# Summing two of three exponential words in GpSimd's accumulating transfers, and a plan without its table

## The chip, the cores and the metric

The kernel runs on one core of a Trainium2 chip. The metric is the device time of one execution in microseconds. Before the change it is 1371.47 us, the median of two runs (1370.7 and 1372.23).

## The reference

Two layers, each of attention and a ReLU feed-forward block, with the same weights in both layers. The sequence has 2048 rows of 512 columns, and there are 32 heads of 16 columns. The feed-forward width is 1792.

```
qkv = (x @ wqkv).reshape(B, S, 3, H, Dh).transpose(2, 0, 3, 1, 4)
q, k, v = qkv[0], qkv[1], qkv[2]
scores = jnp.einsum("bhqd,bhkd->bhqk", q, k) * (Dh ** -0.5)
p = _softmax(scores, axis=-1)
o = jnp.einsum("bhqk,bhkd->bhqd", p, v)
A = o.transpose(0, 2, 1, 3).reshape(B, S, D) @ wo
B = maximum(x @ w1, 0) @ w2

x = x + A(layernorm(x)); x = x + B(layernorm(x))
x = x + A(layernorm(x)); x = x + B(layernorm(x))
```

## The kernel before

**Blocks and slots.** The work of attention is cut into blocks: one head, 128 keys, 512 queries. There are 2 x 4 x 32 x 16 = 4096 of them (chunks of the last layer are narrower, and two or four narrow ones make one block). A slot takes three blocks (W = 3): TensorE writes their scores side by side into one of two PSUM tiles `ps_s` (L1946), and ScalarE takes the exponential of what is in the tile and writes it to a buffer `e` in SBUF (L1959). With 4096 blocks there are 1366 slots.

**Two ways to an exponential.** In a slot, the third block can be left to VectorE. Then ScalarE's exp is 1024 columns wide instead of 1536. VectorE's way uses that the bits of a bf16 number, read as an integer, are nearly its logarithm. One instruction (`first_step`, L1478) adds a bias to the scores and writes them as 16-bit integers into a buffer `lin`. Two such blocks make a pair (GROUP = 2) of 1024 columns in one `lin` buffer. GpSimd then makes two shifted copies with 64-bit integer adds (`shifted`, L1533): `up`, a constant added to each word, and `down`, the constant subtracted. Read as bf16, the sum `lin + up + WEIGHT * down` is close to a multiple of the exponential. The sum is never written: TensorE multiplies each of the three with the values, and adds in PSUM. The weight of `down` lies in scaled copies of the values (`vscaled`, for six of the sixteen key blocks), or is multiplied in by VectorE (`weigh`, L1537).

**Value products.** A product (`pv`, L1299) has 32 output rows, so that four heads' products run side by side, and sums go to one of two PSUM tiles `ps_f` and `ps_o`. A block of ScalarE's takes one product, a block of VectorE's three (PARTS = lin, up, down). When a head group's sums are complete (`finish_segment`), VectorE copies them out; the reciprocal of the softmax's denominator is spread over the rows by transfers of SP and, where there is time, of GpSimd (`widen`, L1253: 64 rows read from four).

**Fillers and repeats.** Projections, transposes and the feed-forward block are cut into small pieces that TensorE does between scores and value products (L429 and others). Where TensorE would stand idle, the scores of a slot are issued more than once (`times`).

**What sets the order.** All instructions are written out in one order by a planner in the kernel's Python. It keeps a clock for each engine (`now_pe`, `now_dve`, `now_pool`, `exp_end`) with assumed costs, and for each slot decides whether VectorE takes a block (only if a `lin` buffer is free, `lin_free`, and GpSimd's queue allows it), which products and fillers TensorE does before the next scores, and when each task of VectorE and GpSimd is issued. A dictionary `rule` holds thresholds of these decisions. A table corrects it: `STARTS` (whether a slot begins a pair), `MORE` and `SLIP` (more fillers, or a shifted limit, in a slot) and `RULES` (new thresholds from a slot on). On the chip each engine follows its own queue in this order and waits for semaphores.

**Buffers.** There are NP = 6 `lin` buffers, NC = 3 of `up` and ND = 4 of `down`. In the old kernel a `lin` buffer is free when both shifts have read it and the value products of `lin` are done; `up` and `down` when their products are done.

Of the kernel before, what the change touches and what calls it, by code (L numbers as in the profile page):

```python
# [12 lines left out]
BF16 = mybir.dt.bfloat16  # L13
# [5 lines left out]
ALU = mybir.AluOpType  # L19
# [7 lines left out]
def kernel(  # L27
# [10 lines left out]
    nc = tc.nc  # L38
# [11 lines left out]
    NKB = S // P  # L50
# [3 lines left out]
    TPC = QS // P  # L54
# [16 lines left out]
    GROUP = 2  # L71
    CHAIN = 1500.0
    NP = 6
    NC = 3
# [15 lines left out]
    CROWDED, POOL_ISSUE, BEHIND = 4500.0, 700.0, 3500.0  # L90
    LOADED, FIRST_LOAD, LATER_LOAD, KEPT_Q = 18000.0, 30, 180, 8
    BOTH = 4
    WHOLE = 4
    STARTS, MORE, SLIP = {27: 0, 33: 0, 22: 0, 38: 1, 52: 0, 57: 0, 61: 0, 79: 0, 98: 0, 100: 1, 103: 1, 107: 1, 128: 1, 136: 0, 158: 1, 193: 0, 220: 1, 239: 0, 221: 0, 260: 1, 242: 1, 251: 0, 249: 0, 305: 1, 301: 1, 325: 1, 323: 1, 351: 0, 368: 1, 366: 0, 392: 1, 401: 1, 402: 0, 418: 0, 405: 1, 438: 1, 456: 0, 477: 1, 516: 0, 505: 1, 533: 1, 526: 0, 595: 1, 659: 0, 642: 0, 681: 0, 693: 0, 710: 0, 708: 0, 740: 1, 753: 0, 755: 1, 746: 0, 749: 0, 769: 0, 765: 1, 799: 1, 806: 0, 815: 1, 830: 1, 838: 0, 829: 0, 869: 1, 866: 0, 873: 1, 880: 0, 883: 0, 881: 1, 907: 1, 902: 0, 953: 0, 960: 0, 985: 0, 991: 0, 1026: 0, 1046: 0, 1068: 0, 1079: 0, 1067: 1, 1076: 1, 1096: 0, 1128: 0, 1125: 0, 1126: 0, 1156: 0, 1158: 0, 1178: 1, 1164: 0, 1189: 0, 1254: 1, 1280: 0, 1370: 0}, {8: 1.0, 2: -1.0, 15: -1.0, 28: 2.0, 42: -1.0, 80: 2.0, 72: -1.0, 95: 1.0, 92: 1.0, 87: -1.0, 156: 1.0, 166: -1.0, 207: 2.0, 223: 2.0, 234: -1.0, 287: 2.0, 318: -1.0, 407: 1.0, 437: 2.0, 495: -1.0, 486: 2.0, 520: 2.0, 533: 1.0, 564: 1.0, 572: 2.0, 577: 1.0, 594: -1.0, 589: 2.0, 599: -1.0, 620: 2.0, 624: 2.0, 649: -1.0, 660: 2.0, 643: 2.0, 669: -1.0, 683: -1.0, 712: 2.0, 736: 2.0, 735: 2.0, 738: 1.0, 741: 2.0, 758: 2.0, 757: 1.0, 786: 2.0, 784: 1.0, 814: 2.0, 819: 1.0, 839: 1.0, 861: 1.0, 874: 1.0, 865: -1.0, 886: 1.0, 897: 1.0, 892: 2.0, 953: 2.0, 955: 1.0, 941: 1.0, 1000: -1.0, 1022: 2.0, 1028: 2.0, 1033: 1.0, 1061: 1.0, 1119: -1.0, 1117: -1.0, 1112: 1.0, 1181: 1.0, 1205: -1.0, 1220: 1.0, 1221: -1.0, 1241: -1.0, 1255: -1.0, 1250: -1.0, 1276: 2.0, 1281: -1.0, 1326: 1.0, 1335: 2.0, 1357: 2.0, 1341: 2.0, 1347: 2.0}, {54: 216.0, 82: -200.0, 141: 216.0, 168: -200.0, 176: 120.0, 180: -200.0, 194: 120.0, 221: 120.0, 249: 120.0, 241: 216.0, 247: 60.0, 279: 120.0, 278: -200.0, 277: 216.0, 282: 216.0, 309: 120.0, 329: 120.0, 355: 216.0, 377: 120.0, 409: 120.0, 432: 120.0, 524: -200.0, 547: 216.0, 552: 216.0, 544: 120.0, 580: 216.0, 616: 60.0, 612: -200.0, 603: -200.0, 644: 60.0, 722: 120.0, 723: -200.0, 730: 60.0, 777: 120.0, 766: 60.0, 763: 60.0, 784: 216.0, 785: -200.0, 792: 216.0, 803: 60.0, 815: 60.0, 819: -200.0, 835: -200.0, 825: 216.0, 830: -200.0, 887: -200.0, 918: -200.0, 909: 216.0, 903: 216.0, 946: 216.0, 951: 120.0, 958: -200.0, 991: 60.0, 1044: 216.0, 1042: -200.0, 1057: 120.0, 1069: 120.0, 1071: 216.0, 1073: 60.0, 1111: 60.0, 1159: 60.0, 1200: 120.0, 1187: 60.0, 1196: 216.0, 1216: 120.0, 1238: 60.0, 1298: 120.0, 1313: 60.0, 1315: -200.0, 1304: -200.0, 1344: 120.0, 1362: -200.0, 1373: 120.0, 1365: 120.0}
# [8 lines left out]
    RULES = {1: {'pressed': 5, 'young': 6}, 21: {'backlog': 4000.0}, 41: {'unit': 360.0, 'pressed': 3, 'hold': 4, 'over': 0.0, 'calm': 1.5, 'cap': 10.0, 'fill': 2000.0, 'rounds': 4}, 61: {'full': 3}, 81: {'unit': 280.0, 'cap': 6.0, 'late': 99.0, 'spare': 10}, 101: {'slack': 300.0, 'fill': 2000.0}, 121: {'margin': 160.0, 'most': 2.0}, 141: {'eager': 0, 'hold': 4, 'late': 3.0, 'rounds': 3, 'pressed': 5, 'margin': 130.0, 'over': 0.0, 'partial': 3}, 161: {'full': 2}, 181: {'full': 2, 'ahead': 3.0, 'calm': 2.0, 'pace': 1.5, 'unit': 320.0, 'partial': 3, 'least': 0.5, 'most': 2.0}, 201: {'far': 2, 'pressed': 3, 'most': 2.0, 'least': 0.5, 'easy': 1.2, 'calm': 3.0, 'near': 8, 'rounds': 4}, 221: {'spare': 20, 'ahead': 3.0, 'calm': 1.2, 'haste': 2.0, 'hold': 4, 'pace': 1.3, 'cap': 3.0, 'young': 4}, 241: {'hold': 4, 'most': 50.0, 'ahead': 5.0, 'haste': 3.0}, 261: {'pressed': 5}, 281: {'cap': 3.0, 'least': 1.0, 'margin': 100.0, 'full': 2}, 301: {'far': 3, 'late': 99.0, 'pressed': 4, 'cap': 3.0, 'backlog': 2200.0, 'calm': 9.0, 'eager': 1, 'unit': 360.0}, 321: {'backlog': 2200.0, 'far': 3, 'eager': 0, 'cap': 6.0, 'unit': 320.0, 'over': 60.0, 'calm': 2.0, 'spare': 14}, 361: {'easy': 1.0, 'late': 2.0}, 381: {'cap': 3.0, 'slack': 300.0}, 401: {'eager': 0, 'pace': 0.7}, 421: {'calm': 9.0, 'old': 4}, 441: {'partial': 2, 'cap': 6.0, 'calm': 1.0, 'fill': 3000.0}, 461: {'pressed': 5}, 481: {'easy': 2.0, 'rounds': 3, 'cap': 10.0, 'pace': 1.0}, 501: {'haste': 1.6, 'ahead': 1.0, 'slack': 300.0, 'least': 1.0}, 521: {'margin': 100.0, 'unit': 360.0}, 541: {'cap': 3.0}, 561: {'closing': 3, 'full': 4}, 581: {'young': 6}, 621: {'partial': 2, 'late': 4.0}, 641: {'ahead': 3.0, 'calm': 1.0}, 661: {'far': 4, 'backlog': 3000.0}, 681: {'calm': 1.2, 'soon': 2000.0, 'unit': 360.0, 'hold': 2, 'far': 2, 'easy': 1.2, 'eager': 1, 'full': 3}, 701: {'young': 4, 'hold': 4}, 721: {'least': 1.0, 'pace': 0.7, 'backlog': 4000.0, 'fill': 3000.0}, 761: {'hold': 2, 'full': 3, 'closing': 6, 'haste': 2.0}, 821: {'over': 120.0, 'partial': 4}, 861: {'pace': 1.5, 'rounds': 3}, 881: {'spare': 6, 'far': 4}, 901: {'backlog': 3000.0}, 941: {'young': 3, 'pace': 1.0, 'far': 4, 'backlog': 3000.0, 'slack': 800.0, 'late': 99.0, 'partial': 2, 'pressed': 5}, 981: {'far': 4, 'slack': 800.0}, 1021: {'ahead': 8.0, 'pace': 0.7, 'rounds': 4, 'near': 6, 'far': 2, 'late': 2.0, 'backlog': 1500.0, 'full': 2}, 1041: {'margin': 60.0, 'young': 4}, 1061: {'margin': 100.0}, 1101: {'old': 4}, 1121: {'rounds': 4}, 1161: {'late': 99.0}, 1201: {'unit': 360.0, 'most': 50.0, 'calm': 1.5, 'over': 200.0, 'full': 4, 'least': 0.5, 'closing': 0, 'cap': 10.0}, 1221: {'margin': 160.0}, 1241: {'calm': 9.0, 'unit': 320.0}, 1261: {'hold': 4}, 1281: {'over': 120.0, 'backlog': 2200.0, 'least': 1.0, 'late': 99.0}, 1301: {'pace': 1.0, 'least': 0.5}, 1321: {'pressed': 4, 'slack': 1300.0}, 1341: {'calm': 1.2, 'unit': 320.0, 'far': 2, 'fill': 2000.0}, 1361: {'slack': 1300.0}}  # L103
# [1015 lines left out]
    for l in range(2):  # L1119


        if l == 0:
            steps = [(0, range(4), 0, TPC), (0, range(4), TPC, 2 * TPC), (0, range(4), 2 * TPC, NKB)]
            steps += [(j, range(4), 0, NKB) for j in range(1, NQS)]
        else:
            steps = [(0, range(4), 0, NKB - TPC), (1, range(NEXT), 0, NKB - TPC)]
            steps += [(0, range(4), NKB - TPC, NKB), (1, range(NEXT, 4), 0, NKB)]
            steps += [(1, range(NEXT), NKB - TPC, NKB)]
            steps += [(j, range(4), 0, NKB) for j in range(2, LAST + 1)]
        for j, Ts, a, b in steps:  # L1130
            for T in Ts:
                sums = acc[8 * j :] if l else acc0
                add_run(l, j, T, range(a, b), load=a and sums, store=b < NKB and sums)
# [246 lines left out]
    def v_round(found, t):  # L1380
# [19 lines left out]
        for p in list(pairs):  # L1400
# [5 lines left out]
            for half in range(GROUP):  # L1406
                line = ("line", p["n"], half)
                if ("read",) + line not in made and not any(x[4] == line for x in p["mms"]):
                    mark(("read",) + line, "pe")
# [57 lines left out]
    PARTS = ("lin", "up", "down")  # L1467
# [5 lines left out]
    def dve_block(half, taken, src, ex, recent):  # L1473
# [27 lines left out]
        for sg, kb, g in taken:  # L1501
# [9 lines left out]
            for part, buf, key, of in (  # L1511
                ("lin", lin[which], line_key, None),
                ("up", up[p["n"] % NC], p["key"] + ("up",), None),
# [7 lines left out]
    def chain(p):  # L1521
# [19 lines left out]
        for of, out, by, war in (  # L1541
# [7 lines left out]
            maker[key + of]["chain"] = p  # L1549
        if not p["scaled"]:  # L1550
            task(quick, weigh, [key + ("down",)], [key + first])
            maker[key + ("down",)]["chain"] = p
# [11 lines left out]
    idle_matmuls(16)  # L1564
# [630 lines left out]
```

## Time and profile before

| what | value |
|---|---|
| profiled execution, its own time | 1371.6 us |
| its span | 1369.8 us |
| TensorE busy | 1333.9 us (97%) |
| ScalarE busy | 1344.5 us (98%) |
| VectorE busy | 1145.0 us (84%) |
| GpSimd busy | 765.7 us (56%) |
| granted TensorE clock | 1.0 |

The span runs from the first to the last instruction of the execution that the profiler recorded. Busy times are unions over the span; issuing a transfer counts as busy on GpSimd, where the profile gives it a length. Four products that run side by side count as one stretch. TensorE's busy time includes the repeated scores. In the rows of groups, a mean length of an exp is longer than the time from one exp to the next, because the end of one overlaps the start of the next.

### The profile page before, as it was taken

What the parts mean: (1) busy time and instruction counts of PE and PEld (TensorE: products, weight loads), DVE (VectorE), ACT (ScalarE), POOL (GpSimd) and SP (SyncE); (2) the same over time, 40 slices, a digit from 0 to 9 for tenths busy, and PEclk for the clock granted to TensorE, in tenths of its full rate; (3) what the DMA queues carried; (4) which work ended last, traced back from release to release, by engine and by line L of the source; (5) the groups of instructions that cost most, each with busy time, mean ns of one, the idle gap of its engine ahead of it and who ended that gap; (6) DMA issues with size and microseconds to landing.
All of it is one profiled execution on the core that took longest, in us unless ns stands there. A gap on an engine that the chain in (4) does not pass through costs nothing. (4 is left out here: it accounts for less than half of the span.)

```text
span 1369.8 us, 48788 instructions
## 1 busy us (share of the span) xinstructions
PE 1333.9 (97%) x20647; PEld 470.5 (34%) x20647; DVE 1145.0 (84%) x1994; ACT 1344.5 (98%) x1437; POOL 765.7 (56%) x1296
## 2 busy tenths in 40 slices
PE   8999999999999999999999999999999999999998
PEld 3222222222222222222222222222234444545665
DVE  7898998869998889986898877998988886887774
ACT  8999999999999999999999999999999999999995
POOL 3456666546566655664566544565545555565441
PEclk9999999999999999999999999999999999999999
DMA  6200012101022100210111100002112211214120
GB/s 148 70 2 14 21 43 45 47 16 33 11 49 48 23 21 6 56 42 18 25 21 32 33 5 6 11 15 52 41 35 51 50 28 38 65 30 96 35 58 19
DMA packets 151579, 50.03 MB, mean 37 GB/s; under 512 B 136608, under 2 KB 148576, under 8 KB 151360
## 3 DMA queue, kind: packets, MB, share of 16 engines
q1 hardware_dynamic: 144832, 41.31, 13.4%
q0 software_dynamic: 5568, 5.15, 2.0%
q8 instruction: 161, 2.64, 0.8%
q10 hardware_dynamic: 960, 0.46, 0.1%
q14 instruction: 58, 0.48, 0.1%
HBM read 24.38 MB, written 2.10 MB: 19 GB/s over the span
## 5 line engine op out<-in xcount | busy, mean ns | idle before, releaser
L1959 ACT ACTIVATE e<-ps_s 128x1024 bf16<-128x1024 f32 (+1 forms) x1366 | 1330.2, 1172 | 6.9 <-PE ps_s L1946 5.1
L1478 DVE TENSOR_SCALAR lin<-ps_s 128x512 int16<-128x512 f32 x1200 | 802.4, 684 | 154.8 <-PE ps_s L1946 116.5
L1533 POOL INT64_ADD up<-lin x600 | 367.6, 617 | 425.6 <-DVE lin L1478 220.7
L1946 PE MATMUL ps_s<-q,ktp 32*128 32x512 bf16 (+2 forms) x5460 | 523.3, 321 | 12.5 <-ACT e L1959 7.6
L1533 POOL INT64_ADD down<-lin x600 | 368.1, 617 | 130.8 <-DVE lin L1478 46.8
L1946 PEld LDWEIGHTS <-ktp 32*128 32x128 bf16 x5728 | 166.5, 91 | 509.4 <-issue 501.1
L1299 PEld LDWEIGHTS <-vaug 128*32 128x32 bf16 x7338 | 178.6, 95 | 196.0 <-issue 167.1
L1299 PE MATMUL ps_o<-e,vaug 128*32 128x512 bf16 (+2 forms) x2094 | 201.3, 321 | 2.6 <-DVE ht L1163 0.8
L1299 PE MATMUL ps_f<-e,vaug 128*32 128x512 bf16 (+2 forms) x1922 | 198.3, 330 | 1.4 <-DVE q L914 0.8
L1299 PE MATMUL ps_f<-lin,vaug 128*32 128x512 bf16 (+2 forms) x766 | 113.8, 332 | 0.1
L1299 PE MATMUL ps_f<-down,vscaled 128*32 128x512 bf16 (+2 forms) x728 | 113.5, 329 | 0.0
L1299 PE MATMUL ps_f<-up,vaug 128*32 128x512 bf16 (+2 forms) x766 | 113.1, 332 | 0.0
L1299 PE MATMUL ps_o<-up,vaug 128*32 128x512 bf16 (+2 forms) x850 | 110.2, 322 | 0.0
L1299 PE MATMUL ps_o<-lin,vaug 128*32 128x512 bf16 (+2 forms) x850 | 105.6, 322 | 0.5 <-DVE ht L1161 0.3
L1299 PE MATMUL ps_o<-down,vscaled 128*32 128x512 bf16 (+2 forms) x798 | 104.7, 320 | 0.0
L1299 PEld LDWEIGHTS <-vscaled 128*32 128x32 bf16 x1526 | 66.8, 96 | 29.2 <-issue 22.0
L429 PE MATMUL ps_o<-w,ht 128*32 128x512 bf16 x896 | 75.4, 383 | 0.6 <-issue 0.5
L429 PE MATMUL ps_f<-w,ht 128*32 128x512 bf16 x784 | 64.5, 383 | 0.2 <-DVE r L1187 0.2
L429 PE MATMUL ps_f<-xnT,w 128*32 128x512 bf16 x688 | 56.6, 383 | 1.5 <-DVE xn L933 1.2
L429 PE MATMUL ps_o<-xnT,w 128*32 128x512 bf16 x656 | 54.1, 383 | 0.1
L429 PEld LDWEIGHTS <-ht 128*32 128x32 bf16 x1680 | 36.5, 95 | 42.8 <-issue 34.8
L429 PE MATMUL ps_o<-xnT,wkq 128*32 128x512 bf16 x496 | 42.7, 383 | 1.7 <-DVE ht L991 0.5
(181 smaller groups left out, 851.9 us busy)
## 6 DMA issues: line engine op xcount, KB each, us to landing
w<-in_B_w_dram SPq DMA_DIRECT2D x144, 128.0 KB
q<-xn SPq DMA_DIRECT2D x36, 64.0 KB
out_dram<-x SPq DMA_DIRECT2D x15, 128.0 KB
x<-in_A_x_dram SPq DMA_DIRECT2D x14, 128.0 KB
ktp<-in_B_w_dram SPq DMA_DIRECT2D x10, 128.0 KB
r<-u POOLq DMA_DIRECT2D x8, 128.0 KB, 4.6
u<-u POOLq DMA_DIRECT2D x8, 128.0 KB, 4.6
xnT<-xn SPq DMA_TRANSPOSE x55
```

Of the source, the lines that this page charges most:

```text
L429: nc.tensor.matmul(G["b"][cols], lhsT[:, cols], rhs, start=not G["begun"][g], stop=not G["cols"][g], tile_position=(0, 32 * g), skip_group ...
L1299: nc.tensor.matmul((ps_f, ps_o)[sg["bank"]][32 * g : 32 * g + 32, 0 : sg["w"]], values[:, 4 * sg["T"] + g, 2 * e : 2 * e + 32], rhs, start ...
L1478: first = nc.vector.tensor_scalar(out=lin[which][:, half * QS : (half + 1) * QS], in0=src, scalar1=EXP_BIAS, scalar2=THIRD, op0=ALU.add, o ...
L1533: nc.gpsimd.int64_add(words(out), words(line), by)
L1946: score = nc.tensor.matmul(b[:, a : a + sg["w"]], kt[32 * g : 32 * g + 32, kc : kc + P], q_home(sg["q"])[32 * g : 32 * g + 32, sg["e"], 0 ...
L1959: ex = nc.scalar.activation(out=eb[:, 0 : place[m]], in_=b[:, 0 : place[m]], func=ACTF.Exp, scale=1.0 / (LOG2E * UNIT),)
```

## The change

After the two shifts, or between them, GpSimd issues a transfer from `lin` to `up` that adds: `up = up + lin`, both read as bf16, 128 partitions of 1024 columns. TensorE then multiplies two words with the values, the sum in `up` and `down`. The `lin` buffer is read by the shifts and the transfer alone. There are four `lin` buffers instead of six and five `up` buffers instead of three. The planner's assumptions are 700 ns on GpSimd for the issue and 4000 ns from there until the sum is there. The table of corrections is emptied, so that the thresholds in `rule` hold throughout. In the first chunk of layer 0, the last three quarters of the keys are taken in two steps for half of the head groups and in one for the others. One of 16 idle products at the start is left out.

```
-    NP = 6
-    NC = 3
+    NP = 4
+    NC = 5
+    ADDED = 4000.0
-    STARTS, MORE, SLIP = {27: 0, 33: 0, 22: 0, ...}, {8: 1.0, 2: -1.0, ...}, {54: 216.0, ...}
+    STARTS, MORE, SLIP = {}, {}, {}
-    RULES = {1: {'pressed': 5, 'young': 6}, 21: {'backlog': 4000.0}, ...}
+    RULES = {}
...
-            steps = [(0, range(4), 0, TPC), (0, range(4), TPC, 2 * TPC), (0, range(4), 2 * TPC, NKB)]
+            steps = [(0, range(4), 0, TPC), (0, range(MID), TPC, 2 * TPC)]
+            steps += [(0, range(MID), 2 * TPC, NKB), (0, range(MID, 4), TPC, NKB)]
...
-            for half in range(GROUP):
-                line = ("line", p["n"], half)
-                if ("read",) + line not in made and not any(x[4] == line for x in p["mms"]):
-                    mark(("read",) + line, "pe")
...
-    PARTS = ("lin", "up", "down")
+    PARTS = ("up", "down")
...
-                ("lin", lin[which], line_key, None),
-                ("up", up[p["n"] % NC], p["key"] + ("up",), None),
+                ("up", up[p["n"] % NC], p["key"] + ("sum",), None),
...
+        def add():
+            nc.gpsimd.dma_start(
+                out=above.bitcast(BF16), in_=line.bitcast(BF16), accum_op=ALU.add
+            )
+            mark(key + ("sum",), "pool", ADDED)
+            for half in range(GROUP):
+                mark(("read", "line", n, half), "pool", ADDED)
+
+        task(POOL_ISSUE, add, [key + ("sum",)], [key + ("up",)], engine="pool")
+        maker[key + ("sum",)]["chain"] = p
...
-    idle_matmuls(16)
+    idle_matmuls(15)
```

More of the change, by code (lines that the diff above doesn't have):

```diff
@@ L93 @@
     WHOLE = 4
-    STARTS, MORE, SLIP = {27: 0, 33: 0, 22: 0, 38: 1, 52: 0, 57: 0, 61: 0, 79: 0, 98: 0, 100: 1, 103: 1, 107: 1, 128: 1, 136: 0, 158: 1, 193: 0, 220: 1, 239: 0, 221: 0, 260: 1, 242: 1, 251: 0, 249: 0, 305: 1, 301: 1, 325: 1, 323: 1, 351: 0, 368: 1, 366: 0, 392: 1, 401: 1, 402: 0, 418: 0, 405: 1, 438: 1, 456: 0, 477: 1, 516: 0, 505: 1, 533: 1, 526: 0, 595: 1, 659: 0, 642: 0, 681: 0, 693: 0, 710: 0, 708: 0, 740: 1, 753: 0, 755: 1, 746: 0, 749: 0, 769: 0, 765: 1, 799: 1, 806: 0, 815: 1, 830: 1, 838: 0, 829: 0, 869: 1, 866: 0, 873: 1, 880: 0, 883: 0, 881: 1, 907: 1, 902: 0, 953: 0, 960: 0, 985: 0, 991: 0, 1026: 0, 1046: 0, 1068: 0, 1079: 0, 1067: 1, 1076: 1, 1096: 0, 1128: 0, 1125: 0, 1126: 0, 1156: 0, 1158: 0, 1178: 1, 1164: 0, 1189: 0, 1254: 1, 1280: 0, 1370: 0}, {8: 1.0, 2: -1.0, 15: -1.0, 28: 2.0, 42: -1.0, 80: 2.0, 72: -1.0, 95: 1.0, 92: 1.0, 87: -1.0, 156: 1.0, 166: -1.0, 207: 2.0, 223: 2.0, 234: -1.0, 287: 2.0, 318: -1.0, 407: 1.0, 437: 2.0, 495: -1.0, 486: 2.0, 520: 2.0, 533: 1.0, 564: 1.0, 572: 2.0, 577: 1.0, 594: -1.0, 589: 2.0, 599: -1.0, 620: 2.0, 624: 2.0, 649: -1.0, 660: 2.0, 643: 2.0, 669: -1.0, 683: -1.0, 712: 2.0, 736: 2.0, 735: 2.0, 738: 1.0, 741: 2.0, 758: 2.0, 757: 1.0, 786: 2.0, 784: 1.0, 814: 2.0, 819: 1.0, 839: 1.0, 861: 1.0, 874: 1.0, 865: -1.0, 886: 1.0, 897: 1.0, 892: 2.0, 953: 2.0, 955: 1.0, 941: 1.0, 1000: -1.0, 1022: 2.0, 1028: 2.0, 1033: 1.0, 1061: 1.0, 1119: -1.0, 1117: -1.0, 1112: 1.0, 1181: 1.0, 1205: -1.0, 1220: 1.0, 1221: -1.0, 1241: -1.0, 1255: -1.0, 1250: -1.0, 1276: 2.0, 1281: -1.0, 1326: 1.0, 1335: 2.0, 1357: 2.0, 1341: 2.0, 1347: 2.0}, {54: 216.0, 82: -200.0, 141: 216.0, 168: -200.0, 176: 120.0, 180: -200.0, 194: 120.0, 221: 120.0, 249: 120.0, 241: 216.0, 247: 60.0, 279: 120.0, 278: -200.0, 277: 216.0, 282: 216.0, 309: 120.0, 329: 120.0, 355: 216.0, 377: 120.0, 409: 120.0, 432: 120.0, 524: -200.0, 547: 216.0, 552: 216.0, 544: 120.0, 580: 216.0, 616: 60.0, 612: -200.0, 603: -200.0, 644: 60.0, 722: 120.0, 723: -200.0, 730: 60.0, 777: 120.0, 766: 60.0, 763: 60.0, 784: 216.0, 785: -200.0, 792: 216.0, 803: 60.0, 815: 60.0, 819: -200.0, 835: -200.0, 825: 216.0, 830: -200.0, 887: -200.0, 918: -200.0, 909: 216.0, 903: 216.0, 946: 216.0, 951: 120.0, 958: -200.0, 991: 60.0, 1044: 216.0, 1042: -200.0, 1057: 120.0, 1069: 120.0, 1071: 216.0, 1073: 60.0, 1111: 60.0, 1159: 60.0, 1200: 120.0, 1187: 60.0, 1196: 216.0, 1216: 120.0, 1238: 60.0, 1298: 120.0, 1313: 60.0, 1315: -200.0, 1304: -200.0, 1344: 120.0, 1362: -200.0, 1373: 120.0, 1365: 120.0}
@@ L102 @@
     }
-    RULES = {1: {'pressed': 5, 'young': 6}, 21: {'backlog': 4000.0}, 41: {'unit': 360.0, 'pressed': 3, 'hold': 4, 'over': 0.0, 'calm': 1.5, 'cap': 10.0, 'fill': 2000.0, 'rounds': 4}, 61: {'full': 3}, 81: {'unit': 280.0, 'cap': 6.0, 'late': 99.0, 'spare': 10}, 101: {'slack': 300.0, 'fill': 2000.0}, 121: {'margin': 160.0, 'most': 2.0}, 141: {'eager': 0, 'hold': 4, 'late': 3.0, 'rounds': 3, 'pressed': 5, 'margin': 130.0, 'over': 0.0, 'partial': 3}, 161: {'full': 2}, 181: {'full': 2, 'ahead': 3.0, 'calm': 2.0, 'pace': 1.5, 'unit': 320.0, 'partial': 3, 'least': 0.5, 'most': 2.0}, 201: {'far': 2, 'pressed': 3, 'most': 2.0, 'least': 0.5, 'easy': 1.2, 'calm': 3.0, 'near': 8, 'rounds': 4}, 221: {'spare': 20, 'ahead': 3.0, 'calm': 1.2, 'haste': 2.0, 'hold': 4, 'pace': 1.3, 'cap': 3.0, 'young': 4}, 241: {'hold': 4, 'most': 50.0, 'ahead': 5.0, 'haste': 3.0}, 261: {'pressed': 5}, 281: {'cap': 3.0, 'least': 1.0, 'margin': 100.0, 'full': 2}, 301: {'far': 3, 'late': 99.0, 'pressed': 4, 'cap': 3.0, 'backlog': 2200.0, 'calm': 9.0, 'eager': 1, 'unit': 360.0}, 321: {'backlog': 2200.0, 'far': 3, 'eager': 0, 'cap': 6.0, 'unit': 320.0, 'over': 60.0, 'calm': 2.0, 'spare': 14}, 361: {'easy': 1.0, 'late': 2.0}, 381: {'cap': 3.0, 'slack': 300.0}, 401: {'eager': 0, 'pace': 0.7}, 421: {'calm': 9.0, 'old': 4}, 441: {'partial': 2, 'cap': 6.0, 'calm': 1.0, 'fill': 3000.0}, 461: {'pressed': 5}, 481: {'easy': 2.0, 'rounds': 3, 'cap': 10.0, 'pace': 1.0}, 501: {'haste': 1.6, 'ahead': 1.0, 'slack': 300.0, 'least': 1.0}, 521: {'margin': 100.0, 'unit': 360.0}, 541: {'cap': 3.0}, 561: {'closing': 3, 'full': 4}, 581: {'young': 6}, 621: {'partial': 2, 'late': 4.0}, 641: {'ahead': 3.0, 'calm': 1.0}, 661: {'far': 4, 'backlog': 3000.0}, 681: {'calm': 1.2, 'soon': 2000.0, 'unit': 360.0, 'hold': 2, 'far': 2, 'easy': 1.2, 'eager': 1, 'full': 3}, 701: {'young': 4, 'hold': 4}, 721: {'least': 1.0, 'pace': 0.7, 'backlog': 4000.0, 'fill': 3000.0}, 761: {'hold': 2, 'full': 3, 'closing': 6, 'haste': 2.0}, 821: {'over': 120.0, 'partial': 4}, 861: {'pace': 1.5, 'rounds': 3}, 881: {'spare': 6, 'far': 4}, 901: {'backlog': 3000.0}, 941: {'young': 3, 'pace': 1.0, 'far': 4, 'backlog': 3000.0, 'slack': 800.0, 'late': 99.0, 'partial': 2, 'pressed': 5}, 981: {'far': 4, 'slack': 800.0}, 1021: {'ahead': 8.0, 'pace': 0.7, 'rounds': 4, 'near': 6, 'far': 2, 'late': 2.0, 'backlog': 1500.0, 'full': 2}, 1041: {'margin': 60.0, 'young': 4}, 1061: {'margin': 100.0}, 1101: {'old': 4}, 1121: {'rounds': 4}, 1161: {'late': 99.0}, 1201: {'unit': 360.0, 'most': 50.0, 'calm': 1.5, 'over': 200.0, 'full': 4, 'least': 0.5, 'closing': 0, 'cap': 10.0}, 1221: {'margin': 160.0}, 1241: {'calm': 9.0, 'unit': 320.0}, 1261: {'hold': 4}, 1281: {'over': 120.0, 'backlog': 2200.0, 'least': 1.0, 'late': 99.0}, 1301: {'pace': 1.0, 'least': 0.5}, 1321: {'pressed': 4, 'slack': 1300.0}, 1341: {'calm': 1.2, 'unit': 320.0, 'far': 2, 'fill': 2000.0}, 1361: {'slack': 1300.0}}
```

## The prediction

> **What bounds the kernel now.** I read the totals and the slices first, then the groups, the waits, the timeline of single stretches, and the DMA issues.
>
> ```profile
> span 1369.8 us, 48788 instructions
> PE 1333.9 (97%) x20647; PEld 470.5 (34%) x20647; DVE 1145.0 (84%) x1994; ACT 1344.5 (98%) x1437; POOL 765.7 (56%) x1296
> ACT  8999999999999999999999999999999999999995
> PEclk9999999999999999999999999999999999999999
> ```
>
> ScalarE is busy from the first slice to the last, and TensorE nearly so, at full granted clock. Which of the two sets the pace is told by the groups and the waits:
>
> ```profile
> L1959 ACT ACTIVATE e<-ps_s 128x1024 bf16<-128x1024 f32 (+1 forms) x1366 | 1330.2, 1172 | 6.9 <-PE ps_s L1946 5.1
> L1478 DVE TENSOR_SCALAR lin<-ps_s 128x512 int16<-128x512 f32 x1200 | 802.4, 684 | 154.8 <-PE ps_s L1946 116.5
> L1533 POOL INT64_ADD up<-lin x600 | 367.6, 617 | 425.6 <-DVE lin L1478 220.7
> L1533 POOL INT64_ADD down<-lin x600 | 368.1, 617 | 130.8 <-DVE lin L1478 46.8
> ```
>
> The 1366 exps fill 1330.2 us, and ScalarE was idle only 6.9 us before them. Nothing else can shorten the program while the exps stay as they are. VectorE and GpSimd have idle time (154.8, and 425.6 and 130.8 us), and it ends when scores or words arrive: they follow.
>
> ```profile
> PE ps_s L1946 <- ACT e L1959: 9.9, 44, 0.5
> DVE lin L1478 <- POOL down L1533: 16.4, 13, 4.5
> ```
>
> These waits show that scores wait for the exp, and that even with six lin buffers VectorE sometimes waits for GpSimd to finish with one (13 times, up to 4.5 us).
>
> Prices of single steps come from the timeline:
>
> ```profile
> 900.66 17.52 ACT L1959 ACTIVATE e<-ps_s 128x1024 bf16<-128x1024 f32 x19 [0.20 <-PE ps_s L1946]
> 30.56 1.46 ACT L1959 ACTIVATE e<-ps_s 128x1536 bf16<-128x1536 f32 x1
> 31.89 0.22 ACT L735 ACTIVATE ya<-va 128x4 f32<-128x4 f32 x1
> 505.91 0.83 PE L429 MATMUL ps_f<-xnT,wkq 128*32 128x512 bf16 x12
> 507.00 0.40 PE L429 MATMUL ps_f<-xnT,wkq 128*32 128x512 bf16 x4
> 271.85 1.26 POOL L1253 DMA_DIRECT2D u<-u x2
> 273.14 1.20 POOL L1533 INT64_ADD up<-lin  x2
> ```
>
> An exp of two blocks costs (17.52 - 1.06) / 18 = 0.914 us from start to start (1.06 is one exp's own length, in the row at 499.64). An exp of three blocks costs 31.89 - 30.56 = 1.33. So each block that VectorE does not take costs ScalarE 0.42 us. A round of four products side by side costs TensorE (0.83 - 0.40) / 2 = 0.215. GpSimd takes 1.29 / 2 = 0.645 per DMA issue and 0.59 per add when they queue.
>
> **The change, part by part.** The instruction order of the two built programs, in which no time stands, gives the counts.
>
> *Blocks.* Before, 1200 blocks are VectorE's and ScalarE runs 1200 exps of two blocks, 165 of three and one of one. After: 1136 and 229, and one. The table is what is missing: the old program with its table emptied has 1112, so the two-product form gives back 24 of the 88 that the table had won. On ScalarE, which sets the end, the 64 blocks cost 64 x 0.42 = **26.6 us**. VectorE saves 64 x 0.68 = 44 us, which lies in its idle time and brings nothing.
>
> *Products.* The lin products go. TensorE had 2896 + 3 x 1200 = 6496 products of 512 columns, and now 2960 + 2 x 1136 = 5232: 316 rounds fewer, 68 us. But the planner repeats score rounds where TensorE would idle, and these rise from 1397 to 1509, 24 us. The net 44 us lie beside ScalarE, which is not released by them. What they can bring is less lateness of scores. The ledger of the old span: 11.0 to the first exp, 1200 x 0.914 + 165 x 1.33 + 0.5 = 1316.7 for exps, 21.9 from the last exp's start (1347.9) to the end; 20.2 is left for 36 normalisation steps on ScalarE (L730 and L735, some 6) and small lateness (14). I keep 20.2: looser TensorE speaks for less, dropped hand corrections for more. If it all went, it would be 14 us less; if it doubled, 14 more.
>
> *GpSimd.* It loses 32 pairs of shifts (x 1.18 = 38 us) and gains 568 issues x 0.645 = 366 us, in all about 1094 us, some 78% of the span. A pair takes 2 x 0.59 + 0.645 = 1.83, and two exps of two blocks take 1.83. In stretches where pairs follow every second slot (477 of 567 intervals) GpSimd is exactly full; each of the 90 longer intervals lets it catch up. Behind an add in its queue stand the next pair's two shifts, and the 48 reciprocal spreads (L1253). I take no loss here; the issue's price is bounded by the issues in the trace, 0.63 below (L1253, 64 rows) and 0.91 above (the weight load at L212 with 512 pieces), and 128 rows are nearer the first.
>
> *The new wait.* The add reads lin, so lin comes free when the add has landed, and lin has four buffers instead of six. VectorE's in-order queue waits at L1478; behind it stand evacuations and the release of the score bank, for which scores and then exps wait. The planner asks only that the add be issued. Call the landing L, from issue. A buffer's round is: the second block's slot 0.92, its lin 0.68, two hand-overs 0.17 each (VectorE's end at 502.32 to GpSimd's start at 502.49), both shifts 1.18, other VectorE work ahead 0.3 (estimate), and L: 3.42 + L. In the new order 282 of 564 rounds have only eight slots, 8 x 0.92 = 7.4 us. So L of up to 4.0 costs nothing, and each us more costs 282 / 4 = 70 us (four chains run side by side). TensorE's reading of the sum has more room: in 95 of 100 pairs it comes eight slots or more after the scores. No accumulating transfer is in the trace; the nearest rows:
>
> ```profile
> r<-u POOLq DMA_DIRECT2D x8, 128.0 KB, 4.6
> r<-u POOLq DMA_DIRECT2D x6, 64.0 KB, 3.1
> q0 software_dynamic: 5568, 5.15, 2.0%
> ```
>
> Per byte, 1.5 us for each 64 KB give 7.6 us for the add's 256 KB; that is the upper end. The lower end is 3.1. The third row is nearer to what happens: 2.0% of 16 engines over the span is 438 engine-us for 48 transfers, 9.1 each, done in some 3 us, so a spread keeps only about three engines at work. It reads four rows sixteen times over; the add has 128 rows on both sides. At 438 us per 5.15 MB, 0.262 MB are 22.3 engine-us, 1.4 us on sixteen engines. With the start of 1.6 (3.1 - 1.5) that is 3.0, and 4.4 if reading the destination doubles the traffic. I take **4.1**: 0.1 x 70 = **7 us**. Traffic is the other bound: 568 x 1.4 to 2.8 us is 58 to 116% of the span on top of 16% now (all queue rows together); 2.8 on each engine against a pair per 1.83 would itself be the limit.
>
> The Trainium skill, DMA: Bandwidth & Descriptors, "Why a DMA increments its semaphore by 16 and not by 1", says that the number of engines follows from the outermost dimension of both sides: the spread's 4 would give four engines, as the trace's three suggest, and the add's 128 give sixteen; the sum by it is the one above, without it 254 us more. The Trainium skill, Collectives: The Full Stack, "The bandwidth ceiling: the fold count and why AG ≠ RS ≠ AR", speaks against this change: an add in a transfer reads two sources through one ring and halves the rate. By it L is 4.4 and the loss 28 us; no run here shows it yet.
>
> *The rest.* Taking the first chunk's keys in fewer steps saves VectorE four stores of sums (0.68 each) in its idle time, and adds nothing to ScalarE, whose blocks are the same; if TensorE were bound there it would gain or lose under 3 us. One idle product less (0.2 us) lies before the first normalisation is ready. Both are taken as nothing.
>
> *Sum.* 11.0 + (1136 x 0.914 + 229 x 1.33 + 0.5 = 1343.4) + 20.2 + 21.9 + 7 = 1403.5; the profiled execution took 1371.6 for a span of 1369.8, so 1.8 is added: **1405 us**. Its own time lies 0.1 us above the median of the runs, 1371.47.
>
> **Rivals.** *The lin loop binds hard* (chance 0.25): the add lands in 4.5 to 5.2 us, because the two reads and other transfers (16% of the engines) delay it. VectorE's lin then waits in half of all rounds: at 4.7, 0.7 x 70 = 49 us, 1447; at 7.6, over 250 us, above 1650. For it: the weight load of 128 rows from GpSimd took 5.3 us in the crowded start. Against: the traffic is otherwise light.
>
> *Looser TensorE makes up for it* (0.27), the other side, not slower: the add lands in under 4.0, nothing is lost in the loop, and of the 14 us of late scores 10 go because TensorE has 44 us less work, so 1405 - 7 - 10 = 1388. It decides once the removed lateness and loop loss together reach 7 us, where the time falls under 1398.9, which is 2% above the old median. For it: scores wait for exps and not the reverse (9.9 against 5.1 us). Against: the 14 us are already about 0.01 us an exp.
>
> *GpSimd is the bound* (0.07): if an issue takes 1.0 instead of 0.645, each dense pair lags 0.35, 477 x 0.35 = 167 us, less one slot of 0.92 or more regained at each of 90 breaks, say 100: 67 us, 1465. For it: GpSimd is exactly full in dense stretches. Against: 629 ns mean for every issue at L1253.
>
> **How the numbers follow.** The forecast holds 0.41, with its own range 1397 to 1420. About 0.05 of it and nearly all of the second rival fall within 2% (which is also about what a measurement of this kernel tells from no change); faster by 2% would need 1344, less than the exps and both ends alone (1376), so 0.01. Slower is the rest, 0.68. The range 1388 to 1480 leaves out lucky ends of the second rival and landings above 5.2.
>
> **What would show it.** Right: 1136 exps of two blocks at 0.91, ScalarE still at 97 to 98%, issues of about 0.65 us on GpSimd, landings of 4 us, DVE lin waiting for DMA less than some 40 us in all, DMA busy near 0.75 to 0.95 of its engines at most. Wrong: landings above 5 us with VectorE's lin waiting for them and gaps before exps ended by PE ps_s; GpSimd above 90% busy; or TensorE's sum products waiting for the transfer; or lateness gone and a time under 1390.

## The result, and the profile after

The changed kernel takes **1661.76 us** (median of 1660.01 and 1663.51) where the kernel before takes 1371.47: the ratio is 1.212, with a 95% interval from 1.206 to 1.218. The forecast was 1405 with a range up to 1480. The direction was right, and 257 us were missing. A run more than 1.5% above the fastest of its kernel is left out of the comparisons; below this concerns one run, of 1684.35 us.

The totals and two rows of slices of the changed kernel:

```profile
span 1661.7 us, 46842 instructions
PE 1468.7 (88%) x19422; PEld 473.8 (29%) x19422; DVE 1125.5 (68%) x1930; ACT 1408.9 (85%) x1436; POOL 1227.4 (74%) x1800
ACT  8997877877786798888989899998789989897985
PEclk9998877988897999999999999998899989997999
```

Before, ScalarE's row read 9 in nearly every slice. Now it has holes everywhere, and no engine reads full in their place: TensorE is at 88%, GpSimd at 74%. So the engines wait for each other. The granted clock of TensorE, 1.0 before, is 0.92 on average. The groups (busy time and mean ns of one, then the idle time before them and what ended most of it):

```profile
L1967 ACT ACTIVATE e<-ps_s 128x1024 bf16<-128x1024 f32 (+1 forms) x1366 | 1393.9, 1124 | 234.1 <-PE ps_s L1954 224.1
L1476 DVE TENSOR_SCALAR lin<-ps_s 128x512 int16<-128x512 f32 x1136 | 755.7, 684 | 370.8 <-DMA up<-lin 155.2
L1530 POOL INT64_ADD up<-lin x568 | 521.8, 919 | 277.4 <-DVE lin L1476 102.4
L1549 POOL DMA_DIRECT2D up<-lin x568 | 568.9, 1002 | 49.9 <-POOL up L1530 34.6
L1530 POOL INT64_ADD down<-lin x568 | 501.9, 900 | 51.8 <-PE ps_o L1301 29.5
```

ScalarE was idle 6.9 us before its exps in the old kernel, and 234.1 now, nearly all of it for scores (224.1). So the question is why scores are late. The waits (total us, times, longest) lead back link by link:

```profile
ACT e L1967 <- PE ps_s L1954: 224.1, 272, 6.4
PE ps_s L1954 <- DVE lin L1476: 106.4, 96, 5.1
DVE lin L1476 <- DMA up<-lin: 155.2, 118, 7.9
POOL up L1530 <- DVE lin L1476: 102.4, 40, 18.8
POOL up L1530 <- PE ps_f L1301: 89.3, 51, 5.9
POOL up L1530 <- PE ps_o L1301: 78.5, 41, 7.0
```

Exps wait for scores; scores wait for VectorE to read the score bank; VectorE waits at `lin` for a buffer that a transfer still reads; and GpSimd, which issues that transfer, waits for TensorE to release `up` (89.3 + 78.5 = 168 us). The chain names links and is not yet a cause: of its last link the old kernel had as much (93.2 + 88.5 = 182 us before the same shift), and there the exps were not late. The old kernel's row:

```profile
L1533 POOL INT64_ADD up<-lin x600 | 367.6, 617 | 425.6 <-DVE lin L1478 220.7 <-PE ps_f L1299 93.2 <-PE ps_o L1299 88.5
```

TensorE's own wait for the sums is small: 4.5 us for `ps_o`, 1.7 for `ps_f`.

The transfers, from the issue row and the queue row:

```profile
up<-lin POOLq DMA_DIRECT2D x568, 256.0 KB, 3.8
q0 software_dynamic: 87360, 154.08, 54.7%
```

The landing is 3.8 us in the median, a little under the 4.1 that the forecast took. Worked out from the 495 of 568 transfers whose landing the trace tells, the mean is 4.0, one in twenty is above 5.4, and the longest takes 7.5.

GpSimd's timeline in a dense stretch (start, length):

```profile
203.27 1.12 POOL L1549 DMA_DIRECT2D up<-lin  x1
203.90 1.16 POOL L1530 INT64_ADD up<-lin  x1
204.49 1.15 POOL L1530 INT64_ADD down<-lin  x1
205.35 1.11 POOL L1549 DMA_DIRECT2D up<-lin  x1
205.96 1.17 POOL L1530 INT64_ADD up<-lin  x1
206.54 1.16 POOL L1530 INT64_ADD down<-lin  x1
207.43 1.11 POOL L1549 DMA_DIRECT2D up<-lin  x1
```

The issues end at 204.39, 206.46 and 208.54: a pair takes **2.08 us**, not 1.83. Rows overlap (an instruction starts before the one ahead has ended), so read prices from end to end: the shift after an issue starts 0.6 us behind it, but ends at 205.06 instead of about 204.5. Two shifts alone take 1.17 when they queue, so an accumulating issue makes a pair 2.08 - 1.17 = **0.91** longer (in these rows 0.82 of it lie before the end of the issue, the rest in the shift behind it).

The round of a `lin` buffer, from the first write into it to its release (sum landed and both shifts done), worked out from single instructions: 9.0 us in the median, where half of the rounds have 7.4. The part that is far from the forecast is the time from the end of `lin` to the start of the first shift: 1.8 us in the median and 3.2 at three quarters, against 0.17 in the forecast. In the old kernel's trace the same time is 0.2 and 1.6.

### The profile page after: what moved, and what is told of

The parts are those of the page before. It is cut to its first block, busy times and chain, and to the rows that moved or that the text cites. A ratio compares the mean times of both kernels' runs of the same rounds, so it can differ in the third digit from the quotient of the medians.

```text
span 1661.7 us, 46842 instructions
## 1 busy us (share of the span) xinstructions
PE 1468.7 (88%) x19422; PEld 473.8 (29%) x19422; DVE 1125.5 (68%) x1930; ACT 1408.9 (85%) x1436; POOL 1227.4 (74%) x1800
## 3 DMA queue, kind: packets, MB, share of 16 engines
q0 software_dynamic: 87360, 154.08, 54.7%
## 5 line engine op out<-in xcount | busy, mean ns | idle before, releaser
L1967 ACT ACTIVATE e<-ps_s 128x1024 bf16<-128x1024 f32 (+1 forms) x1366 | 1393.9, 1124 | 234.1 <-PE ps_s L1954 224.1
L1476 DVE TENSOR_SCALAR lin<-ps_s 128x512 int16<-128x512 f32 x1136 | 755.7, 684 | 370.8 <-DMA up<-lin 155.2
L1954 PE MATMUL ps_s<-q,ktp 32*128 32x512 bf16 (+2 forms) x5857 | 634.3, 338 | 118.5 <-DVE lin L1476 94.2
L1530 POOL INT64_ADD up<-lin x568 | 521.8, 919 | 277.4 <-DVE lin L1476 102.4
L1549 POOL DMA_DIRECT2D up<-lin x568 | 568.9, 1002 | 49.9 <-POOL up L1530 34.6
L1530 POOL INT64_ADD down<-lin x568 | 501.9, 900 | 51.8 <-PE ps_o L1301 29.5
L1301 PEld LDWEIGHTS <-vaug 128*32 128x32 bf16 x5780 | 150.6, 96 | 346.2 <-issue 325.1
L1301 PE MATMUL ps_o<-e,vaug 128*32 128x512 bf16 (+2 forms) x2210 | 231.3, 343 | 5.5 <-DVE ht L1165 1.6
L1954 PE MATMUL ps_s<-w,ktp 32*128 32x512 bf16 x339 | 54.9, 436 | 16.2 <-DVE lin L1476 12.3
L430 PE MATMUL ps_f<-xnT,wkq 128*32 128x512 bf16 x608 | 55.4, 405 | 2.0 <-DVE ktp L859 0.9
```

The costliest lines, as they stand in the source:

```text
L430: nc.tensor.matmul(G["b"][cols], lhsT[:, cols], rhs, start=not G["begun"][g], stop=not G["cols"][g], tile_position=(0, 32 * g), skip_group ...
L1301: nc.tensor.matmul((ps_f, ps_o)[sg["bank"]][32 * g : 32 * g + 32, 0 : sg["w"]], values[:, 4 * sg["T"] + g, 2 * e : 2 * e + 32], rhs, start ...
L1476: first = nc.vector.tensor_scalar(out=lin[which][:, half * QS : (half + 1) * QS], in0=src, scalar1=EXP_BIAS, scalar2=THIRD, op0=ALU.add, o ...
L1530: nc.gpsimd.int64_add(words(out), words(line), by)
L1549: nc.gpsimd.dma_start(out=above.bitcast(BF16), in_=line.bitcast(BF16), accum_op=ALU.add)
L1954: score = nc.tensor.matmul(b[:, a : a + sg["w"]], kt[32 * g : 32 * g + 32, kc : kc + P], q_home(sg["q"])[32 * g : 32 * g + 32, sg["e"], 0 ...
```

## The experiments

All times are medians, and ratios are to the kernel before in the same group of runs. Theories of the first group: A, the `lin` loop (landing, and how late the add is issued); B, GpSimd's time per issue; C, TensorE's clock; D, the plan without its table.

### No transfer, and the old program without its table

```
-            nc.gpsimd.dma_start(
-                out=above.bitcast(BF16), in_=line.bitcast(BF16), accum_op=ALU.add
-            )
```

This is the changed kernel in the same order, with the `lin` word missing from the sum.

> The changed kernel in its own order, with the adding transfer left out: the products read up without the lin word in it, so that word's part of the sum is missing. Theory A (landing): lin comes free only when the transfer has landed, in 4.0 us mean and 5.4 us in one of twenty, and four buffers are too few for that. Theory B (GpSimd): a dense pair takes GpSimd 2.06 us instead of 1.83, because descriptors are written there. Both expect that the loss is gone here: 1395 to 1405, granted clock 1.0. Theory D (plan): the order by rules alone is what is slow; then the time stays above 1550.

Measured: 1404.09 us, ratio 1.024 [1.018, 1.029]. ScalarE is full again:

```profile
L1964 ACT ACTIVATE e<-ps_s 128x1024 bf16<-128x1024 f32 (+1 forms) x1366 | 1357.5, 1231 | 16.3 <-PE ps_s L1951 13.1
```

So 1661.76 - 1404.09 = 258 us hang on the transfers, and the plan without its table is not their cause (D falls). The forecast's other terms come within 6 us of this number: 1405 less the 7 us of the loop is 1398.

The other run is the old kernel with `STARTS, MORE, SLIP` and `RULES` empty, with three products.

> The kernel before with its table emptied and nothing else: 1112 blocks on VectorE instead of 1200. ScalarE's ledger gives 88 x 0.42 = 37 us more: 1400 to 1420, clock 1.0. Theory D (plan): above 1500.

Measured: 1422.69, ratio 1.037 [1.034, 1.040], 3 us above the expectation. With the same rules, two products for three gain 1422.7 - 1404.1 = 18.6 us (batches shared): 24 blocks x 0.42 = 10 of it on ScalarE; the other 9 are less lateness by the forecast's ledger. Without its transfer, the new form would be the better one.

### A narrow add, and a plain copy

```
-                out=above.bitcast(BF16), in_=line.bitcast(BF16), accum_op=ALU.add
+                out=above.bitcast(BF16)[:, 0:64], in_=line.bitcast(BF16)[:, 0:64], accum_op=ALU.add
```

Only 64 of the 1024 columns are added.

> The changed kernel, with the transfer adding only the first 64 of 1024 columns; the lin word is missing from the other sums. The issue on GpSimd and its 128 rows stay, the bytes and so the landing shrink (to some 2.2 us). Theory A: 1400 to 1440, since a buffer's round of 3.4 + 2.2 fits eight slots of 0.92. Theory B: GpSimd's pairs still take 2.06, so the time stays above 1560.

Measured: 1550.78, ratio 1.131 [1.119, 1.142]. The landing is 2.3 us instead of 3.8. The dense pair stays at 2.08 (worked out from the ends of its issues), so an issue's price does not come from its bytes. The time lies between the numbers of A and B, just under B's: neither is the whole cause.

```
-            nc.gpsimd.dma_start(
-                out=above.bitcast(BF16), in_=line.bitcast(BF16), accum_op=ALU.add
-            )
+            nc.gpsimd.dma_start(out=above.bitcast(BF16), in_=line.bitcast(BF16))
```

The copy overwrites the `up` word.

> The changed kernel, with the transfer copying lin over up instead of adding, so that the up word is missing from the sum. Issue on GpSimd and bytes stay; a row is read once, and its packet should take 0.08 us (as on SP's queue) instead of 0.185: landing near 3 us. Theory A: at least half of the loss is gone, 1410 to 1520. Theory B: above 1580.

Measured: 1519.69, ratio 1.108 [1.102, 1.114]. Its queue, its issue, its landing and GpSimd's timeline:

```profile
q0 software_dynamic: 51008, 154.08, 28.5%
...
L1549 POOL DMA_DIRECT2D up<-lin x568 | 317.4, 559 | 51.1 <-POOL up L1530 33.3
...
up<-lin POOLq DMA_DIRECT2D x568, 256.0 KB, 2.4
```

```profile
210.29 0.56 POOL L1549 DMA_DIRECT2D up<-lin  x1
...
212.03 0.56 POOL L1549 DMA_DIRECT2D up<-lin  x1
```

The same shape without the add has an issue of 0.56 us, a pair of 1.74, a landing of 2.4, and half the transfer time: 28.5% of 1520.7 us is 433 us on each engine, 54.7% of 1661.7 is 909, for the same 154.08 MB. The time is the upper end of what theory A gave. But the expectation took the issue's price to stay, and it fell to 0.57 of a pair, so the run does not test the landing alone. It does show that GpSimd's price is not the whole: with pairs below 1.83, GpSimd is not over-full, and still 116 us are lost over the kernel without transfer. VectorE waits 92.5 us for the copies at `lin`, and `lin` stands 1.6 us (median) ahead of its first shift.

### The copy on SyncE's queue

```
-            nc.gpsimd.dma_start(out=above.bitcast(BF16), in_=line.bitcast(BF16))
+            nc.sync.dma_start(out=above.bitcast(BF16), in_=line.bitcast(BF16))
```

This is against the copy above, to free GpSimd of the issue.

> As the plain copy from GpSimd (1520 us), but the copy is issued on SP's queue, so GpSimd has only its two shifts (1.17 us a pair instead of 1.74); the up word is missing from the sum. If GpSimd's queue is the larger part of a buffer's round: 1405 to 1440. If the landing is: above 1480.

Measured: 1632.65, ratio 1.191 [1.175, 1.207], with GpSimd at 44%. The number is on the side of the landing, but it doesn't tell the theories apart, for it moved the wait to another in-order queue. The waits of SP's own queue:

```profile
SPq L1549 <- POOL up L1530: 386.8, 253, 9.6
SPq L1193 <- DVE lin L1476: 151.1, 46, 9.3
```

SP stands behind one copy's shift while the next copies and the spreads of the reciprocals (L1193) are behind it. What it does show: an idle GpSimd is no cure when the release of `lin` stands behind other waits.

### Issues alone, and a transfer that does not hold `lin`

```
+            nc.gpsimd.dma_start(out=spare_out[n % 8][:], in_=spare_in[:], accum_op=ALU.add)
```

In place of the add, 568 accumulating transfers of 128x32 between spare buffers that nobody uses (they are made and set to zero once; those lines are left out here).

> The changed kernel in its own order, with 568 accumulating transfers of 128 rows by 32 columns between two spare buffers that nothing else reads or waits for; the lin word is missing from the sum. GpSimd pays every issue (dense pair 2.06 us), nobody waits for a landing. Theory B: above 1520, near the narrow add's 1551. Theory A': 1405 to 1450.

Measured: 1470.65, ratio 1.071 [1.068, 1.075]. GpSimd's timeline:

```profile
199.76 3.38 POOL L1549 DMA_DIRECT2D spare_out<-spare_in  x1
...
201.81 3.42 POOL L1549 DMA_DIRECT2D spare_out<-spare_in  x1
...
203.86 3.45 POOL L1549 DMA_DIRECT2D spare_out<-spare_in  x1
```

They seem three times as long, but they end at 203.14, 205.23 and 207.31, again 2.08 apart: here nothing makes an issue wait for the shift ahead of it, so rows start earlier and overlap more. GpSimd's price is that of the changed kernel, and with next to no bytes to move it costs 1470.65 - 1404.09 = **67 us** (batches differ by under 3 us in the kernel before). The time lies between the theories' numbers. The shifts start late here too, 1.6 us in the median and 3.1 at three quarters behind `lin` (0.8 and 2.2 without any transfer): the backlog comes with the issues, not with the landing.

```
-                out=above.bitcast(BF16), in_=line.bitcast(BF16), accum_op=ALU.add
+                out=above.bitcast(BF16), accum_op=ALU.add,
+                in_=wv[:].rearrange("p c f -> p (c f)")[:, 0 : GROUP * QS],
```

The full add, with weights as its source, so that `lin` comes free at the shifts.

> The changed kernel in its own order, its transfer adding the first two rows of wv to up instead of lin, so that the sum has another word in it. Issue on GpSimd (1.0 us), bytes, landing and the waits for the sum stay; only lin is no longer held until the landing, VectorE's lin writes wait for the two shifts alone. Theory A' (VectorE held at lin by the landing is the path on which the loss reaches ScalarE): 1410 to 1480. Theory B (GpSimd's queue is over-full, whatever lin waits for): above 1560.

Measured: 1535.22, ratio 1.118 [1.107, 1.130], landing 3.9; this too lies between the theories' numbers. So 64 us more than the issues alone for transfers of full size, whose landing the products of `up` wait for. TensorE's waits for these sums are 9.7 + 6.8 us; where the rest of the 64 arises no run separates. And from here to the changed kernel, **127 us** for the one thing that is left, that `lin` is held until the landing. GpSimd's waits for TensorE before the first shift are 44.5 + 26.3 = 71 us here, against the 168 of the changed kernel.

### A fifth `lin` buffer

```
-    NW1 = 4
+    NW1 = 3
...
-    NP = 4
+    NP = 5
```

The room is taken from a weight buffer.

> The changed kernel with five lin buffers instead of four (and three w1 buffers instead of four, to make room). 1138 blocks, and most rounds of a buffer now have ten slots, 9.2 us at full pace, where the changed kernel's rounds took 9.0 us in the median and had eight slots, 7.4 us. Theory A (a buffer's whole round, GpSimd's queue and landing together): the loss of 258 us against the kernel without the transfer falls to half or less, 1460 to 1535. Theory B (GpSimd's 2.06 us a dense pair alone): lag is the same, above 1600.

Measured: 1654.68 (one run), 7 us under 1661.76, which is no clear gain. That is in the range of theory B, though GpSimd's price alone makes only 67 us. VectorE still waits:

```profile
DVE lin L1476 <- DMA up<-lin: 146.8, 117, 6.1
```

With a fifth buffer, the planner fills it and the shifts start still later: 3.9 us (median) behind `lin` instead of 1.8. A buffer ahead of an engine that is behind becomes queue.

### The plan knows the landing, or the price, or both

The planner asks of a buffer only that its add has been issued (`in made`). This edit asks that by its clock the add has landed and both shifts are done, at most 0.5 us from now, and sets the issue to 1000 ns:

```
-    CROWDED, POOL_ISSUE, BEHIND = 4500.0, 700.0, 3500.0
+    CROWDED, POOL_ISSUE, BEHIND = 4500.0, 1000.0, 3500.0
...
-            ("read", "line", n, half) in made
-            and all(("e", n, of) in made for of in ("up", "down"))
+            (at([("read", "line", n, half)], "dve") or 1e18) <= now_pe[0] + 500.0
+            and all((at([("e", n, of)], "dve") or 1e18) <= now_pe[0] + 500.0 for of in ("up", "down"))
```

> The changed kernel with the whole add, planned with the issue's true price (1000 ns instead of 700) and with a lin buffer counted free only when the plan has its landing behind it (not when the add is issued). The plan gives VectorE 1010 blocks; ScalarE's ledger is 1396 for exps and 64 for the rest, 1460. Theories A and B, and the clock as a follower of the stalls: 1450 to 1490, clock above 0.99. If stalls have another source: above 1550.

Then the second half alone (1000 ns, blind to the landing), the first half alone (700 ns), and both with five buffers:

> The changed kernel with the issue's true price in the plan (1000 ns instead of 700) and nothing else: 1066 blocks, ledger 1437; eight-slot rounds of a lin buffer 102 instead of 282. If GpSimd's price in the plan is what matters: 1440 to 1500, less than the 1509 of the plan that also waits for the landing. If the plan's blindness to the landing matters: 1530 or more.

> The plan that knows the landing, with the issue priced at 700 ns as in the changed kernel: 1040 blocks, ledger 1447. If the plan's blindness to the landing is the larger part of the loss and the price of 700 ns the smaller: 1490 to 1560. If both are needed: 1570 to 1640.

> The plan that knows the landing and the issue's price (1509 us), with five lin buffers instead of four (and three w1 buffers). The plan gives VectorE 1076 blocks instead of 1010, ledger 1433 instead of 1460. If a fifth buffer did not help the changed kernel because GpSimd was over-full and its queue took up the room: here, with the queue short, it helps, 1450 to 1500. If lin buffers are not what is scarce: 1509 or more.

| plan | blocks | exps and 61 us | measured | ratio | lateness |
|---|---|---|---|---|---|
| blind, 700 ns (the changed kernel) | 1136 | 1404 | 1661.8 | 1.212 [1.206, 1.218] | 258 |
| blind, 1000 ns | 1066 | 1433 | 1633.6 | 1.190 [1.178, 1.203] | 200 |
| landing known, 700 ns | 1040 | 1444 | 1495.4 | 1.092 [1.088, 1.095] | 51 |
| landing known, 1000 ns | 1010 | 1457 | 1509.4 | 1.101 [1.098, 1.105] | 53 |
| landing known, 1000 ns, five buffers | 1076 | 1429 | 1488.9 | 1.085 [1.082, 1.088] | 60 |

The third column is the forecast's ledger: 0.914 for each exp of two blocks, 1.33 for each of three, and 61 us for the rest, which is what the kernel without transfer needed (1404.1 - 1343.4). The last column is what is left. Knowing the landing takes away 207 of 258, or 147 of 200 us of lateness, and costs 24 to 40 us in blocks that VectorE no longer takes. Knowing the price takes away 58 us of lateness in the blind plan, at 29 us in blocks, and nothing once the landing is known. An obvious rival is that these plans only give GpSimd sparser pairs. The counts speak against it: two slots lie between 389 of 532 pairs in the blind plan with 1000 ns, and 350 of 519 in the plan that knows the landing with 700 ns; eight-slot rounds of a `lin` buffer, though, fall from 102 to 1. Three of the four expectations held; the plan with both missed its range by 19 us. Three waits of the version with 700 ns:

```profile
POOL up L1530 <- DVE lin L1476: 285.9, 175, 17.3
...
ACT e L1967 <- PE ps_s L1954: 49.3, 69, 3.5
...
DVE lin L1476 <- DMA up<-lin: 2.5, 2, 1.5
```

GpSimd now waits for VectorE, no longer the reverse; VectorE's wait for the add has gone from 155.2 us to 2.5, and 49.3 us of late exps are about the lateness that is left. Traffic alone does not explain the lateness: this version keeps the engines of the queue busier (56.3% of its span, 54.7% in the changed kernel), at a landing of 3.9. From `lin` to its first shift it is 0.1 us in the median, as the forecast had assumed. The fifth buffer, worth nothing in the blind plan, now allows 66 more blocks (28 us by the ledger) and gains 20. None of these versions beats the kernel before.

### TensorE's clock

The trace shows TensorE's clock at half in 45 stretches of 3.4 to 17 us, 259 us in all (none before). Counted from exp to exp, the changed kernel's exps start 287 us later than their own lengths ask (21 before, 30 without transfer); 150 of the 287 us arose in these stretches and 137 outside. Is the clock a cause? If gaps lower it, a kernel with other amounts of repeated scores should move. With the transfer left out and no repeats:

```
-    STREAMED, WINDOW = 0.56, 3413.0
+    STREAMED, WINDOW = 0.0, 3413.0
```

> The kernel without the transfer (1404 us; the lin word is missing from the sum), and without repeated scores: 1365 score rounds instead of 1509, 1146 blocks. It has no transfer to wait for, only less work on TensorE. Theory C (the clock is a cause of its own: TensorE just below some share of activity falls to half clock, and then cannot hold a slot of 0.91 us): 1420 to 1500, with clock 0.90 to 0.98. If the clock only follows: 1395 to 1410.

Measured: 1406.32, ratio 1.026 [1.023, 1.029], at a mean clock of 0.98: 2 us over the run with repeats, 6 over its own ledger (1146 blocks, 1400). And the changed kernel with more repeats (0.95 in that place):

> The changed kernel, planned to repeat scores until TensorE streams 0.95 of a 3.4 us window instead of 0.56: 2204 score rounds instead of 1509, and 1052 blocks (ledger 35 us more). Theory C (about half of the lost time arises because each stall drops the clock to half for 3.4 us or more): clock above 0.97 and 1540 to 1600. If the clock only mirrors the stalls: 1640 or more.

Measured: 1679.64, ratio 1.224 [1.209, 1.239], at 0.95: nothing gained in time; 35 us are more exps (1052 blocks), so the lateness is 241 us instead of 258. The clock did not rise above the 0.97 that the expectation asked for, so this run can't settle it.

Each of the 45 stretches lasts a whole number of windows of 3.41 us. The Trainium skill, TensorE: Matmul & The Clock Gate, "HAM oscillation — how this bites in real kernels", says that a wait which crosses a window of about 3.4 us halves the clock. The trace agrees with the length of the window, but not with the wait: in the 3.41 us before a stretch TensorE was busy for 2 to 78% (57% in the median), and the longest gap there was 1.3 us in the median and never filled the window. Cut into such windows, this trace has none with TensorE busy for less than 62% that kept the full clock, so many short gaps do it too (the ends of products are modelled in the trace, so the shares are rough).

What the clock costs no run isolates. At a mean of 0.98 without transfer it did next to no harm. Whether it lengthens the stalls once they are there stays open: in the changed kernel the two always come together.

## Why the prediction was wrong, step by step

**Blocks and exps: right.** 1136 exps of two blocks; the ledger without the loop gives 1398, and the kernel without transfer took 1404.

**Products: small, as said.** Two for three gained 18.6 us under equal rules, 10 of it through blocks that the count had already included. The second rival (looser TensorE, 1388) fell: even without any transfer the time stayed at 1404.

**GpSimd: the price was taken from the wrong end of its bounds.** The step bounded an issue by 0.63 and 0.91 and chose 0.645, by the likeness in rows. It took 0.91. A plain copy of the same shape takes 0.56, so the add, not the shape, decides. A pair then needs 2.08 where two exps leave 1.83, and "exactly full" becomes over-full. The rival "GpSimd is the bound" put this at 67 us with an issue of 1.0, and the run with issues alone measured 67 with 0.91. Its mechanism held, with a chance of 0.07, but as one part of three. That the numbers are the same is partly luck: by the rival's own working an issue of 0.91 lags 477 x 0.265 = 126 us, and the 100 that it let the breaks regain would leave 26.

**Landing: right.** 3.8 in the median against 4.1 taken. Traffic, the other bound, did not bind: 909 us for 568 transfers are 1.6 on each engine, within the 1.4 to 2.8 of the forecast, against a pair per 2.08. The Trainium skill, Collectives: The Full Stack, "The bandwidth ceiling: the fold count and why AG ≠ RS ≠ AR", spoke against the change because an add reads two sources. The trace agrees: 909 us of transfer time instead of 433 for the plain copy, and 3.8 us instead of 2.4. The Trainium skill gives the rule for a reduction among cores; here it holds inside one core's SBUF. That 256 KB landed sooner than the 128 KB of the old spreads (4.6 us) agrees with the sixteen engines that the forecast had taken. (The forecast's "254 us more" without sixteen engines is a small slip: by its own slope, 7.6 in place of 4.1 gives 3.5 x 70 = 245.)

**The new wait: the step that failed.** The formula 3.42 + L put 0.17 us for the hand-over from VectorE to GpSimd, which is the price for an idle GpSimd, read from one row; the old trace had 0.2 in the median and 1.6 at three quarters. The add stands in the same in-order queue as shifts that wait for `up` and `down` to come free, and this queue is not empty: 1.8 us in the median and 3.2 at three quarters. Put in place of 0.17, 1.8 gives a round of 3.42 - 0.17 + 1.8 + 3.8 = 8.9 us (measured 9.0) against 7.4. By the step's own 70 us per us this is 1.5 x 70 = 105 us, where holding `lin` until the landing measured 127. The slope was about right: from the narrow add to the full one, 1.5 us more of landing cost 111 us, 74 per us, with more traffic in it. The kink was not: "L of up to 4.0 costs nothing", but a landing of 2.3 already cost 80 us more than issues alone. The two faults may also feed each other: a late queue holds `lin` longer, the wait for `lin` delays scores, late scores delay value products, and these release `up`, for which the queue waits. This ring is argued from the waits, not shown; for it speaks that GpSimd waited 71 us for TensorE before the first shift where `lin` was not held, and 168 where it was. No run shows one cause for the sum. The runs show a ladder in one and the same order: 67 us for issues, 64 for the full transfer (for which the forecast had no term), 127 for holding `lin`.

**Why the plan didn't see it.** The forecast named it ("the planner asks only that the add be issued") and then priced it with rounds alone. The table of plans above shows this blindness to be the largest single piece: an order that waits for the landing loses 51 to 53 us in lateness instead of 200 to 258.

**Small costs taken as nothing** (the first chunk's steps, the idle product) were not run alone; all that the other terms missed is the 6 us by which 1404 differs from 1398. "TensorE's reading of the sum has more room" was right: 6.2 us of waits.

## What to carry to other kernels

When a buffer's release is moved behind an in-order queue, price the round with the queue's backlog, not with the hand-over of an idle engine, and look at its late quarter as well as its median. "Exactly full" is no cover: an issue that takes 0.27 us more than assumed, on an engine without slack, has already cost 5% here, and a further buffer gives that engine only a longer queue. A plan that frees a buffer at the issue of its reader, instead of at the landing, writes the wait into the order of every engine; letting the plan know the landing was worth 124 to 166 us here, with transfers of the same kind and 28 to 48 fewer of them.

## What the runs showed of the hardware

- An accumulating transfer of 128 rows costs GpSimd 0.91 us to issue, for 8, 16 or 256 KB alike (a pair of 2.08 us each time); the plain copy of 128x1024 bf16 costs 0.57 by the same reading (1.74 - 1.17).
- Its rows begin before the ones ahead have ended: in the changed kernel shifts of 617 ns show means of 919 and 900, with issues alone 1585 and 1545, at one and the same pair of 2.08 us. On this engine, lengths of rows must not be added up; ends must be compared.
- TensorE's clock went to half for 1 to 5 windows of 3.41 us at a time, at a busy share of 88%, and stayed at 1.0 before at 97%. It needed no gap as long as a window: the longest gap in the window ahead was 1.3 us in the median.
